# Windowed attention with a gate, decode step: one collecting matmul a pair, sums of probabilities applied once a set, gate inputs accumulated in strided column groups

## The chip, the cores and the metric

The kernel runs on one core of a Trainium2 chip. The metric is device time in microseconds of one execution, here the median of three runs. The profile and the trace come from one further execution, whose own time is in the table below. Five engines work from queues of their own and meet at semaphores: PE (matrix products into PSUM, with PEld for the loading of weights), DVE and ACT (elementwise work and reductions), POOL (a few memsets here) and SP, which issues nearly all loads. All data are 32-bit floats.

## The reference

Two tokens (B = 2, one position each) of width 512. Attention over the last 4096 positions of a cache of 32768, with 32 query heads on 8 key/value heads, and a gated MLP beside it:

```python
x = A_x                                   # (2, 1, 512)
xn = _layernorm(x)
# attention: W = 4096, rep = 4, Dh = 128
q = (xn @ wq).reshape(B, 1, 32, 128).transpose(0, 2, 1, 3)
k = jnp.repeat(k_cache[:, :, Sk - W:, :], 4, axis=1)
v = jnp.repeat(v_cache[:, :, Sk - W:, :], 4, axis=1)
p = _softmax(jnp.einsum("bhqd,bhkd->bhqk", q, k) * 128 ** -0.5)
s = jnp.einsum("bhqk,bhkd->bhqd", p, v).transpose(0, 2, 1, 3).reshape(B, 1, 4096) @ wo
# gate: w_in (512, 1792), halves of 896
z = _gelu(xn @ w_in)
z1, z2 = z[..., :896], _layernorm(z[..., 896:])
g = _silu((z1 * (w_sp * z2 + b_sp)) @ w_out)
return x + s * g
```

## The kernel before

Work goes by *pairs*: a pair is one batch entry and one key/value head, 16 in all (pair n is batch n // 8, head n % 8). A pair needs 2 MB of keys and 2 MB of values. All large loads are issued by SP in the order of use into a ring of nine slots of 16 KB a partition (`slot`): w_in in two halves, w_out, wq in four, then k and v of each pair, then wo in seven blocks. A slot is loaded anew when the matmuls that read it have ended.

Every instruction of PE, DVE, ACT and SP is recorded through one helper (`InOrder`), which keeps the program order of the source on each engine. So the source order is the queue order, and the profile shows nearly everything at line 36, the helper's; groups are told apart by their tiles. A full matmul of 32-bit floats shows as two records in the profile, a transpose on PE as one.

The preamble (lines 85 to 276) normalizes x, makes the gate inputs `z` (lines 182 to 193), turns them (`zT_ps`, lines 198 to 202), computes the gate (lines 218 to 264) with the queries in between, and turns the queries into `qT`.

The loop over pairs (lines 413 to 435) runs three pairs at once: `cur` (keys turned, scores, row maximum), `prev` (exponent, transposed probabilities, product with the values, evacuation) and `old` (collection). In one iteration:

- `bias` and `probs` of prev: the negative maximum (DVE), then the exponent on ACT, which also leaves the row sums `p.l`
- `transposes` of cur: 32 PE transposes of keys into `kt` banks, copied to `kts` by DVE or ACT; between them `probs_t` of prev, two DVE transposes of the probabilities
- `share_sum` and `weights` of prev: PE adds the row sums over partitions, DVE takes the reciprocal and makes four scales `p.w`
- `scores` of cur: 16 matmul passes into four column groups of `s`
- `collect` of old: four matmuls of 128 columns add the parts of the evacuated output `p.o` into `col`, one column group for each 32 of the 128 columns of a head; if the pair is the last of its set, DVE reduces `col` into `o1`
- `pv` of prev, `row_max` and `share_max` of cur, `evacuate` of prev on ACT, with the scales `p.w`

The output projection works on *sets* of heads: set 0 is heads 0 to 3, set 1 heads 4 and 5, set 2 heads 6 and 7, of both batch entries (`SETS`). So set 0 ends with pairs 3 and 11, set 1 with pairs 5 and 13, set 2 with pairs 7 and 15, and `collect` of pair 13 stands in the iteration of pair 15. `spread` brings a finished set into the form `oT` that the product with wo needs: matmuls with 0/1 matrices (`perm8`, `perm16`) and one DVE copy.

After the loop (lines 460 to 495) come, in this order: bias and exponent of pair 15, spread of sets 0 and 1, the DVE transposes of pair 15's probabilities, collection of pair 14, the sums and weights of pair 15, and then alternately the halves of `pv` of pair 15 and the wo blocks, `collect` of pair 15, `spread(2)`, the third wo block, the evacuation `parts` and the last product `so`:

```python
    bias(last)
    probs(last)
    spread(0)
    spread(1)
    probs_t(last, 0)
    probs_t(last, 1)
    collect(old)
    ...
    wo_early(1)
    collect(last)
    spread(2)
    wo_early(2)
```

Of the kernel before, what the change touches and what calls it, by code (L numbers as in the profile page):

```python
# [9 lines left out]
F32 = mybir.dt.float32  # L10
# [4 lines left out]
P = 128  # L15
HQ, DH = 32, 128
G = 4
# [24 lines left out]
def kernel(  # L42
# [38 lines left out]
    def bank(name, *shape):  # L81
        return ps.tile([P, *shape], F32, tag="kt", name=name, bufs=3)
# [82 lines left out]
    heads = cst.tile([P, 32, REP], F32, tag="heads", name="heads")  # L165
    dve.tensor_copy(heads, free_ap(rowm, 0, [[0, 32], [8, REP]]))
# [3 lines left out]
    perm8 = cst.tile([P, 4, 8, 4, 4], F32, tag="perm8", name="perm8")  # L170
    nc.gpsimd.memset(perm8, 0.0)
    for x in range(4):
        dve.tensor_copy(perm8[:, x, :, :, x], free_ap(ident, 0, [[1, 8], [32, 4]]))
    perm16 = cst.tile([P, 2, 16, 4, 2], F32, tag="perm16", name="perm16")
    nc.gpsimd.memset(perm16, 0.0)
    for x in range(2):
        dve.tensor_copy(perm16[:, x, :, :, x], free_ap(ident, 0, [[1, 16], [32, 4]]))
# [3 lines left out]
    assert KT == G  # L181
    z = sb.tile([P, F], F32, tag="kts", name="z")
    for n in range(G):
        pz = bank(f"z{n}", 512)[:, :FC]
        for k in range(KT):
            pe.matmul(
                pz[32 * k : 32 * k + 32, :], xnT[:, k, :], win[k // 2][:, k % 2, n * FC : (n + 1) * FC],
                start=True, stop=True,
            )
        if n % 2:  # L190
            dve.tensor_copy(z[:, n * FC : (n + 1) * FC], pz)
        else:
            act.activation(z[:, n * FC : (n + 1) * FC], pz, AF.Copy)
# [4 lines left out]
    pt = bank("zT_ps", 2, FT, B)  # L198
    zv = z.rearrange("b (h p j) -> b h j p", h=2, j=FT)
# [19 lines left out]
    dve.tensor_copy(zT, pt)  # L219
# [31 lines left out]
    queries(2)  # L251
    y = bank("y", DC)
    for j in range(FT):
        for g in range(G):
            pe.matmul(
                y[32 * g : 32 * g + 32, :], hT[:, j, :], wout[:, j, g * DC : (g + 1) * DC],
                start=(j == 0), stop=(j == FT - 1),
            )
# [31 lines left out]
    for i, (kv, n, nj) in enumerate(SETS):  # L290
        o1 = cst.tile([P, B, 32], F32, tag=f"o1_{i}", name=f"o1_{i}")
# [4 lines left out]
        sets[f"oT{i}"] = (o1, oT, nj)  # L296

# [80 lines left out]
    def collect(p):  # L378
        b, kv = divmod(p.n, HKV)
        a0, n, o1 = sets[kv]  # L380
        if a0 == 0:
            col[b] = ps.tile([P, 4, 32], F32, tag="col", name=f"col{p.n}")
        for a in range(4):
            pe.matmul(
                col[b][32 * a : 32 * a + 32], selw[:, 28 - REP * a0 : 60 - REP * a0], p.o[:, :, 32 * a : 32 * a + 32],
                start=(a0 == 0), stop=(a0 == n - 1),
            )
        if a0 == n - 1:
            dve.reduce_sum(o1[:, b, :], col[b].rearrange("p a j -> p j a"), axis=AX.X)

    def spread(i):
        o1, oT, nj = sets[f"oT{i}"]
        perm = {8: perm8, 16: perm16}[nj]
        nx = 32 // nj
        pt = bank(f"oT_ps{i}", B, nj)
        for x in range(nx):
            pe.matmul(
                pt, perm[:, x].rearrange("p h a x -> p (h a x)"), o1[:, :, nj * x : nj * x + nj],
                start=(x == 0), stop=(x == nx - 1),
            )  # L400
        dve.tensor_copy(oT[:, :, 0 : 16 * B : 16], pt.rearrange("p b j -> p j b"))
# [11 lines left out]
    for cur in pairs:  # L413
# [11 lines left out]
        do(share_sum, prev)  # L425
        do(weights, prev)
# [41 lines left out]
    share_sum(last)  # L468
    weights(last)
# [54 lines left out]
```

## Time and profile before

| | us |
|---|---|
| median of 3 runs | 219.26 (219.24 to 219.27) |
| the profiled execution | 219.47 |
| its span, first to last instruction | 217.6 |
| PE busy | 175.8 (81%) |
| DVE busy | 109.7 (50%) |
| ACT busy | 80.5 (37%) |
| read from HBM | 89.40 MB, mean 411 GB/s over the span |

In the prediction's lines, a timeline row gives start, duration, engine, source line, operation, tiles (out<-in), shapes and a count of merged records; in square brackets stands the idle time of the engine before the row and what ended it. PE's ends are modelled, so starts are the safer times. A row of the chain in order of time gives start, duration and what the chain consisted of. A row of a table by stretches gives, after the stretch and its length, the busy time and the records of PE, PEld, DVE, ACT and POOL, then the granted clock of PE, the share of the DMA engines' time and GB/s.

### The profile page before, as it was taken

How to read it: one execution, taken by the hardware profiler on the slowest of the kernel's cores; microseconds unless marked ns; L12 is line 12 of the kernel's file. 1: busy time of each engine (PE TensorE's matmuls, PEld its weight loads, DVE VectorE, ACT ScalarE, POOL GpSimd, SP SyncE). 2: the span in 40 equal slices, each digit the busy share in tenths (PEclk: the TensorE clock that was granted, in tenths of full speed). 3: DMA queues.
4: the chain of work that ended last, by engine and by line, in shares of the span. 5: the costliest groups of instructions: out<-in, count | busy, mean ns of one | idle time of the engine just before them, and what ended most of it. 6: DMA issues, size and time to landing. Idle time of an engine off the chain costs nothing.

```text
span 217.6 us, 3810 instructions
## 1 busy us (share of the span) xinstructions
PE 175.8 (81%) x1554; PEld 106.3 (49%) x1554; DVE 109.7 (50%) x259; ACT 80.5 (37%) x173; POOL 3.6 (2%) x17
## 2 busy tenths in 40 slices
PE   0479986676997999797977979797986899798963
PEld 0127623436572846455462746456372847464232
DVE  2411225653774557575664747575663557476001
ACT  5011230032373336435363544536363236444210
POOL 6000000000000000000000000000000000000000
PEclk9998599996999699999999999999999699999999
DMA  6999999999999999999999999999999999999980
GB/s 241 428 439 425 434 434 431 431 426 419 428 434 428 434 429 428 431 434 431 434 434 428 431 425 431 434 429 425 425 428 431 431 435 426 431 431 428 423 332 11
DMA packets 6673, 89.64 MB, mean 412 GB/s; under 512 B 750, under 2 KB 766, under 8 KB 1152
## 3 DMA queue, kind: packets, MB, share of 16 engines
q1 hardware_dynamic: 6636, 89.40, 96.6%
q8 instruction: 12, 0.20, 0.3%
q14 instruction: 5, 0.04, 0.0%
q10 hardware_dynamic: 20, 0.01, 0.0%
HBM read 89.40 MB, written 0.00 MB: 411 GB/s over the span
## 4 chain that ended last, share of the span: by engine, by line
DMA 88%; PE 9%; issue 0%; DVE 0%
DMA k<-in_A_k_cache_dram 65%; DMA wq<-in_A_wq_dram 11%; DMA wo<-in_A_wo_dram 9%; PE kt L36 8%; DMA win<-in_B_w_in_dram 3%; PE q_ps L36 1%; DVE res L36 0%; PE so L36 0%; PE mo L36 0%
## 5 line engine op out<-in xcount | busy, mean ns | idle before, releaser
L36 PE MATMUL kt<-ident,k 128*128 128x128 f32 x512 | 69.8, 291 | 19.1 <-DMA k<-in_A_k_cache_dram 19.1
L36 PEld LDWEIGHTS kt<-ident,k 128*128 128x128 f32 x512 | 59.7, 148 | 26.9 <-issue 18.6
L36 DVE COPY kts<-kt 128x512 f32<-128x512 f32 x64 | 42.4, 681 | 30.5 <-PE kt L36 18.3
L36 ACT ACTIVATE kts<-kt 128x512 f32<-128x512 f32 x64 | 36.7, 597 | 37.9 <-PE kt L36 37.9
L36 ACT ACTIVATE o<-acc,wd 128x128 f32<-128x128 f32 x64 | 18.3, 368 | 54.4 <-PE acc L36 37.7
L36 PE MATMUL acc<-v,pT 128*16 128x512 f32 x256 | 30.6, 593 | 0.4 <-DVE pT L36 0.4
L36 PE MATMUL s<-kts,qT 128*32 128x512 f32 x256 | 30.8, 598 | 0.0
L36 DVE TENSOR_REDUCE m<-s 128x1 f32<-128x1024 f32 x16 | 19.6, 1222 | 13.5 <-PE s L36 13.5
L36 DVE STREAM_TRANSPOSE pT<-p 128x512 f32<-128x512 f32 x32 | 20.7, 686 | 0.2 <-ACT p L36 0.2
L36 ACT ACTIVATE p<-s,nb 128x1024 f32<-128x1024 f32 x16 | 18.1, 1133 | 3.7 <-DVE nb L36 3.7
L36 PEld LDWEIGHTS acc<-v,pT 128*16 128x16 f32 x256 | 7.8, 108 | 10.7 <-issue 10.3
L36 PEld LDWEIGHTS mo<-mg,same 128*128 128x128 f32 x32 | 4.8, 188 | 15.9 <-DVE mg L36 15.9
L36 PEld LDWEIGHTS s<-kts,qT 128*32 128x32 f32 x256 | 6.6, 108 | 10.0 <-ACT kts L36 7.9
L36 PE MATMUL q_ps<-wq,xnT 128*32 128x512 f32 x64 | 9.0, 687 | 1.7 <-DMA wq<-in_A_wq_dram 1.7
L36 PE MATMUL z<-win,xnT 128*32 128x448 f32 x32 | 7.2, 907 | 2.8 <-DMA win<-in_B_w_in_dram 2.8
L36 PEld LDWEIGHTS col<-o,selw 128*32 128x32 f32 x128 | 4.1, 110 | 9.0 <-issue 8.7
L36 DVE TENSOR_REDUCE o<-col 128x32 f32<-128x128 f32 x6 | 1.8, 292 | 12.4 <-PE col L36 12.4
L36 PE MATMUL mo<-mg,same 128*128 128x4 f32 x32 | 6.2, 263 | 2.1 <-DVE mg L36 1.6
L36 DVE TENSOR_REDUCE nb<-mo 128x1 f32<-128x4 f32 x16 | 2.6, 162 | 9.9 <-PE mo L36 9.9
L36 PE MATMUL part<-wo,oT 128*32 128x512 f32 x48 | 5.7, 596 | 1.4 <-DMA wo<-in_A_wo_dram 1.3
L36 PE MATMUL zT_ps<-rowm,z 128*128 128x2 f32 x28 | 6.6, 370 | 0.0
L36 PEld LDWEIGHTS zT_ps<-rowm,z 128*128 128x128 f32 x28 | 6.5, 325 | 0.0
(98 smaller groups left out, 82.1 us busy)
## 6 DMA issues: line engine op xcount, KB each, us to landing
k<-in_A_k_cache_dram SPq DMA_DIRECT2D x16, 2048.0 KB, 34.6
v<-in_A_v_cache_dram SPq DMA_DIRECT2D x16, 2048.0 KB, 36.1
wq<-in_A_wq_dram SPq DMA_DIRECT2D x4, 2048.0 KB, 21.1
wo<-in_A_wo_dram SPq DMA_DIRECT2D x3, 2048.0 KB, 33.7
win<-in_B_w_in_dram SPq DMA_DIRECT2D x2, 1792.0 KB, 9.1
wout<-in_B_w_out_dram SPq DMA_DIRECT2D x1, 1792.0 KB, 14.8
wo<-in_A_wo_dram SPq DMA_DIRECT2D x1, 1024.0 KB, 32.2
wo<-in_A_wo_dram SPq DMA_DIRECT2D x1, 512.0 KB, 28.9
```

The costliest lines, as they stand in the source:

```text
L36: return self.tc.keep_in_program_order(call(*args, **kwargs))
```

## The change

- **Sums of probabilities once a set.** `share_sum` and `weights` are gone. The exponent leaves its row sums in a column of `lsum`. `evacuate` scales by the constant selector `diag`. A new function `normalize`, called by `collect` at the last pair of a set, adds the sums of all the set's pairs with one matmul, reduces `col`, picks each head's sum, takes the reciprocal and scales `o1`.
- **One collecting matmul a pair.** `collect` issues one matmul of 512 columns into 32 rows of `col` in place of four of 128 into four column groups. `o1` is now (heads of the set) x batch x 128; the reduction over the four parts reads 512 elements a row and writes 128.
- **Spreading.** One matmul of 256 columns with a fan-out matrix, two DVE products with a selector (`own`), and one DVE reduction of 256 elements replace the `perm` matmuls and the copy.
- **Gate.** `z` is accumulated over the four parts of x in PSUM, in four column groups whose columns are strided by 7 in w_in; one ACT evacuation; four PE transposes in place of 14 matmuls; two copies into `zT`. `y` takes 7 matmuls of 512 columns, an evacuation and 4 matmuls with `rowm`, in place of 28 of 128.

```diff
@@ gate inputs
-    for n in range(G):
-        pz = bank(f"z{n}", 512)[:, :FC]
-        for k in range(KT):
+    z = sb.tile([P, P, 4], F32, tag="kts", name="z")
+    pz = bank("z_ps", 512)
+    for k in range(KT):
+        for g in range(G):
+            first = FH * (g // 2) + (FT - 4) * (g % 2)
             pe.matmul(
-                pz[32 * k : 32 * k + 32, :], xnT[:, k, :], win[k // 2][:, k % 2, n * FC : (n + 1) * FC],
-                start=True, stop=True,
+                pz[32 * g : 32 * g + 32, :], xnT[:, k, :], free_ap(win[k // 2], F * (k % 2) + first, [[FT, P], [1, 4]]),
+                start=(k == 0), stop=(k == KT - 1),
             )
...
+    act.activation(z.rearrange("p q j -> p (q j)"), pz, AF.Copy)
...
-    for h in range(2):
-        for j in range(FT):
-            pe.matmul(pt[:, h, j, :], zv[:, h, j, :], rowm[:, :B], start=True, stop=True)
+    pt = bank("zT_ps", 4, P)
+    for j in range(4):
+        pe.transpose(pt[:, j, :], z[:, :, j], ident)
@@ output of the gate
+    yp = bank("yp", D)
+    for j in range(FT):
+        g = j % G
+        pe.matmul(yp[32 * g : 32 * g + 32, :], hT[:, j, :], wout[:, j, :], start=(j < G), stop=(j >= FT - G))
+    ys = sb.tile([P, D], F32, tag="o", name="ys")
+    act.activation(ys, yp, AF.Copy)
     y = bank("y", DC)
-    for j in range(FT):
-        for g in range(G):
-            pe.matmul(
-                y[32 * g : 32 * g + 32, :], hT[:, j, :], wout[:, j, g * DC : (g + 1) * DC],
...
+    for g in range(G):
+        pe.matmul(y[32 * g : 32 * g + 32, :], rowm, ys[:, g * DC : (g + 1) * DC], start=True, stop=True)
@@ probabilities
-        p.l = sb.tile([P, 1], F32, tag="l", name=f"l{p.n}")
...
-            bias=p.nb, scale=SCALE, accum_out=p.l,
+            bias=p.nb, scale=SCALE, accum_out=lsum[:, p.n : p.n + 1],
...
-    def share_sum(p):
-        pe.matmul(p.mo[:, G : G + 1], heads.rearrange("p a h -> p (a h)"), p.l, start=True, stop=True)
-
-    def weights(p):
-        w = sb.tile([P, 1], F32, tag="w", name=f"w{p.n}")
-        dve.reciprocal(w, p.mo[:, G : G + 1])
-        p.w = sb.tile([P, 4], F32, tag="wd", name=f"wd{p.n}")
-        dve.tensor_scalar_mul(p.w, diag, w)
@@ evacuate
-            act.activation(p.o[:, jj, :], acc[:, jj, :], AF.Copy, scale=p.w[:, jj : jj + 1])
+            act.activation(p.o[:, jj, :], acc[:, jj, :], AF.Copy, scale=diag[:, jj : jj + 1])
@@ collect
-        for a in range(4):
-            pe.matmul(
-                col[b][32 * a : 32 * a + 32], selw[:, 28 - REP * a0 : 60 - REP * a0], p.o[:, :, 32 * a : 32 * a + 32],
-                start=(a0 == 0), stop=(a0 == n - 1),
-            )
+        pe.matmul(
+            col[b][:32].rearrange("p a d -> p (a d)"), selw[:, 28 - REP * a0 : 60 - REP * a0],
+            p.o.rearrange("p a d -> p (a d)"), start=(a0 == 0), stop=(a0 == n - 1),
+        )
         if a0 == n - 1:
-            dve.reduce_sum(o1[:, b, :], col[b].rearrange("p a j -> p j a"), axis=AX.X)
+            normalize(p.n, n, o1)
+
+    def normalize(last, n, o1):
+        b, m = last // HKV, n * REP
+        pl = bank(f"l{last}", n)
+        pe.matmul(
+            pl[:32], heads.rearrange("p a h -> p (a h)"), lsum[:, last + 1 - n : last + 1], start=True, stop=True
+        )
+        dve.reduce_sum(o1[:, b, :], col[b][:m].rearrange("p a d -> p d a"), axis=AX.X)
+        lm = sb.tile([m, n], F32, tag=f"lm{n}", name=f"lm{last}")
+        dve.tensor_mul(lm, pl[:m], diag[:m, :n])
+        w = sb.tile([m, 1], F32, tag=f"w{n}", name=f"w{last}")
+        dve.reduce_sum(w, lm, axis=AX.X)
+        dve.reciprocal(w, w)
+        dve.tensor_scalar_mul(o1[:, b, :], o1[:, b, :], w)
@@ spread
-        for x in range(nx):
-            pe.matmul(
-                pt, perm[:, x].rearrange("p h a x -> p (h a x)"), o1[:, :, nj * x : nj * x + nj],
-                start=(x == 0), stop=(x == nx - 1),
-            )
-        dve.tensor_copy(oT[:, :, 0 : 16 * B : 16], pt.rearrange("p b j -> p j b"))
+        nx = DH // nj
+        pt = bank(f"oT_ps{i}", B, nx, nj)
+        pe.matmul(
+            pt.rearrange("p b x j -> p (b x j)"), fan[nx].rearrange("p h x -> p (h x)"),
+            o1.rearrange("p b d -> p (b d)"), start=True, stop=True,
+        )
+        t = sb.tile([P, B, nx, nj], F32, tag="fan", name=f"fan_{i}")
+        for b in range(B):
+            dve.tensor_mul(t[:, b], pt[:, b], free_ap(own[nx], 0, [[1, nx], [0, nj]]))
+        dve.reduce_sum(oT[:, :, 0 : 16 * B : 16], t.rearrange("p b x j -> p j b x"), axis=AX.X)
```

In the loop and after it, the calls of `share_sum` and `weights` are dropped; the order of the other calls is the same.

More of the change, by code (lines that the diff above doesn't have):

```diff
@@ L164 @@
     dve.tensor_copy(same, free_ap(rowm, 0, [[0, G], [1, 32]]))
-    heads = cst.tile([P, 32, REP], F32, tag="heads", name="heads")
-    dve.tensor_copy(heads, free_ap(rowm, 0, [[0, 32], [8, REP]]))
+    heads = cst.tile([P, 8, REP], F32, tag="heads", name="heads")
+    dve.tensor_copy(heads, free_ap(rowm, 0, [[0, 8], [8, REP]]))
     diag = cst.tile([P, 4], F32, tag="diag", name="diag")
@@ L169 @@
     dve.tensor_reduce(selw[:, 28:32], free_ap(rowm, 0, [[1, REP], [4, 4]]), axis=AX.X, op=ALU.add)
[L170 to L182, printed above, removed]
-    for n in range(G):
-        pz = bank(f"z{n}", 512)[:, :FC]
-        for k in range(KT):
+    fan, own = {}, {}
+    for nx in (8, 16):
+        fan[nx] = cst.tile([P // nx, P // nx, nx], F32, tag=f"fan{nx}", name=f"fan{nx}")
+        dve.tensor_copy(fan[nx], free_ap(ident[: P // nx], 0, [[1, P // nx], [0, nx]]))
+        own[nx] = cst.tile([P, nx], F32, tag=f"own{nx}", name=f"own{nx}")
+        dve.tensor_reduce(own[nx], ident.rearrange("p (h x) -> p x h", x=nx), axis=AX.X, op=ALU.add)
+    assert G == 4 and 4 < FT < 9
+    z = sb.tile([P, P, 4], F32, tag="kts", name="z")
[3 more added lines that the diff above has]
+            first = FH * (g // 2) + (FT - 4) * (g % 2)
             pe.matmul(
-                pz[32 * k : 32 * k + 32, :], xnT[:, k, :], win[k // 2][:, k % 2, n * FC : (n + 1) * FC],
-                start=True, stop=True,
-            )
[L190 to L193, printed above, removed]
+                pz[32 * g : 32 * g + 32, :], xnT[:, k, :], free_ap(win[k // 2], F * (k % 2) + first, [[FT, P], [1, 4]]),
+                start=(k == 0), stop=(k == KT - 1),
+            )
+    act.activation(z.rearrange("p q j -> p (q j)"), pz, AF.Copy)
     wb_ps = ps.tile([P, 512], F32, tag="mo", name="wb_ps")[:, :2]
@@ L218 @@
     zT = cst.tile([P, 2, FT, B], F32, tag="zT", name="zT")
-    dve.tensor_copy(zT, pt)
+    for m, j0, j1 in ((0, 0, 4), (1, 4, FT)):
+        src = free_ap(pt, 32 * m + P * (j0 - (FT - 4) * m), [[64, 2], [P, j1 - j0], [1, B]])
+        dve.tensor_copy(zT[:, :, j0:j1, :], src)
     u = cst.tile([P, 2, FT, B], F32, tag="u", name="u")
@@ L381, in collect @@
         if a0 == 0:
-            col[b] = ps.tile([P, 4, 32], F32, tag="col", name=f"col{p.n}")
-        for a in range(4):
-            pe.matmul(
-                col[b][32 * a : 32 * a + 32], selw[:, 28 - REP * a0 : 60 - REP * a0], p.o[:, :, 32 * a : 32 * a + 32],
-                start=(a0 == 0), stop=(a0 == n - 1),
-            )
-        if a0 == n - 1:
-            dve.reduce_sum(o1[:, b, :], col[b].rearrange("p a j -> p j a"), axis=AX.X)
+            col[b] = ps.tile([P, 4, DH], F32, tag="col", name=f"col{p.n}")
```

14 lines of the change are left out of this document (2 added, 12 removed).

## The prediction

> **What bounds the kernel now.** I read the chain of waits first, on the page and then in order of time, because it says which work ended last at each moment.
>
> ```profile
> DMA 88%; PE 9%; issue 0%; DVE 0%
> ...
> q1 hardware_dynamic: 6636, 89.40, 96.6%
> q8 instruction: 12, 0.20, 0.3%
> ```
>
> ```profile
> 153.05 35.68 DMA k<-in_A_k_cache_dram
> 188.73 0.14 issue
> 188.86 4.14 PE kt L36 x32
> ...
> 213.51 0.04 issue
> 213.55 0.47 PE so L36 x8
> ```
>
> The load queue fills 96.6% of its engines' time, and the chain is loads but for short pieces. So work saved in the sixteen pairs is worth nothing by itself: the same 89.40 MB must still come. What can move the end is the stretch after the last keys landed at 188.73 (pair 15). From there the compute has one pass through scores, probabilities, values, collection and output, while the last loads (v15 and the blocks of wo) still arrive until 213.51. I therefore read the timeline of each engine from 188.86, PE first.
>
> ```profile
> 188.86 4.14 PE L36 MATMUL kt<-ident,k 128*128 128x128 f32 x32 [1.32 <-DMA k<-in_A_k_cache_dram]
> 192.84 0.28 PE L36 MATMUL mo<-l,heads 128*128 128x1 f32 x2
> 193.05 1.92 PE L36 MATMUL s<-kts,qT 128*32 128x512 f32 x16
> 194.79 0.40 PE L36 MATMUL col<-o,selw 128*32 128x128 f32 x8
> 195.01 1.90 PE L36 MATMUL acc<-v,pT 128*16 128x512 f32 x16
> 197.01 0.39 PE L36 MATMUL mo<-mg,same 128*128 128x4 f32 x2
> ...
> 200.01 1.07 PE L36 MATMUL acc<-v,pT 128*16 128x512 f32 x8 [0.36 <-DVE pT L36]
> 200.90 1.90 PE L36 MATMUL part<-wo,oT 128*32 128x512 f32 x16
> 202.62 1.04 PE L36 MATMUL acc<-v,pT 128*16 128x512 f32 x8
> 203.78 1.92 PE L36 MATMUL part<-wo,oT 128*32 128x512 f32 x16
> 205.52 0.40 PE L36 MATMUL col<-o,selw 128*32 128x128 f32 x8
> 206.33 1.06 PE L36 MATMUL oT_ps<-o,perm 128*128 128x16 f32 x8 [0.41 <-DVE o L36]
> 208.72 1.92 PE L36 MATMUL part<-wo,oT 128*32 128x512 f32 x16 [1.33 <-DMA wo<-in_A_wo_dram]
> ...
> 211.66 1.71 PE L36 MATMUL so<-wo,oT 128*32 128x128 f32 x56
> 213.55 0.43 PE L36 MATMUL so<-wo,oT 128*32 128x128 f32 x8 [0.18 <-DMA wo<-in_A_wo_dram]
> ```
>
> ```profile
> 195.26 0.29 DVE L36 TENSOR_REDUCE o<-col 128x32 f32<-128x128 f32 x1 [1.40 <-PE col L36]
> 195.47 1.22 DVE L36 TENSOR_REDUCE m<-s 128x1 f32<-128x1024 f32 x1
> 196.72 0.23 DVE L36 TENSOR_SCALAR mg<-grpm,m 128x4 f32<-128x4 f32 x1
> 197.43 0.16 DVE L36 TENSOR_REDUCE nb<-mo 128x1 f32<-128x4 f32 x1 [0.48 <-PE mo L36]
> 197.62 0.15 DVE L36 TENSOR_SCALAR nb<-nb 128x1 f32<-128x1 f32 x1
> ...
> 199.25 1.31 DVE L36 STREAM_TRANSPOSE pT<-p 128x512 f32<-128x512 f32 x2 [0.21 <-ACT p L36]
> ...
> 214.04 0.29 DVE L36 TENSOR_TENSOR res<-so,gate 128x128 f32<-128x128 f32 x1 [6.36 <-PE so L36]
> ```
>
> ```profile
> 196.98 1.14 ACT L36 ACTIVATE o<-acc,wd 128x128 f32<-128x128 f32 x4 [3.34 <-DVE mg L36]
> 197.99 1.13 ACT L36 ACTIVATE p<-s,nb 128x1024 f32<-128x1024 f32 x1
> ```
>
> The slack of this stretch is what the change must not use up. Pair 15's second half of values starts at 202.62, and its eight passes issue in 0.89 (200.01 to 200.90), so PE was free at 203.51 and stood 0.27 until 203.78. At 208.72 it stood 1.33 for wo. The 56 passes of so from 211.66 are seven blocks of eight; eight passes took 0.22 elsewhere (194.79 to 195.01), so the last block could have gone at 211.66 + 7 x 0.22 = 213.20 and waited 0.35. Together 0.27 + 1.33 + 0.35 = 1.95 us.
>
> **The change part by part.** Removed from every pair: the sum of shares on PE (0.21, from 192.84 to 193.05), the reciprocal and the scaling on DVE (two small operations), and three of four collecting matmuls. None of it ended a wait of the load queue, so by itself it gives nothing before pair 15.
>
> *The preamble* (gate inputs, four turning transposes, y in two steps) ends under the loads: PE waits for keys at every pair, 19.1 us over the kernel.
>
> ```profile
> L36 PE MATMUL kt<-ident,k 128*128 128x128 f32 x512 | 69.8, 291 | 19.1 <-DMA k<-in_A_k_cache_dram 19.1
> L36 PE MATMUL zT_ps<-rowm,z 128*128 128x2 f32 x28 | 6.6, 370 | 0.0
> L36 PE MATMUL z<-win,xnT 128*32 128x448 f32 x32 | 7.2, 907 | 2.8 <-DMA win<-in_B_w_in_dram 2.8
> ```
>
> The turning falls from 28 passes (6.6 us) to 4; the 32 passes of z now read with a stride, which no row shows. Even at twice 7.2 us they add about what the turning gives back. I count 0; with the cover gone the preamble would be worth -6 to +1. Gate is used only at 214.04.
>
> *The collecting matmul.* A call is two records here (64 calls, x128). Before, eight passes of 128 columns over four column groups took 0.22. Now two passes of 512 columns run in one group. Sixteen 512-column passes over four groups go from 200.90 to 202.62: 1.72, four rounds of 0.43. A lone pass costs at least a quarter of a round, 0.11, and at most a round. The 32 transposes, one at a time, take 4.14 for 128 columns each, 0.13, or 0.52 for 512, so I take the whole round: 2 x 0.43 = 0.86 (bounds 0.22 and 1.04). The Trainium skill, "TensorE: Matmul & The Clock Gate", section "Back-to-back issue gap", gives 216 ns for 512 columns; by it the matmul would cost 0.43, each of the two on the path below would be 0.43 cheaper, and the sum would be +0.3 instead of +1.2. The rounds of 0.43 at full clock speak against it.
>
> *Normalizing once a set* is the new work on DVE: a reduction of 512 elements in place of 128, then four small dependent operations. Between 0.29 for 128 elements and 1.22 for 1024 the line gives 0.69 for 512 (bounds 0.29 and 1.22). DVE takes the next independent operation about 0.08 before the end (195.26 + 0.29 against 195.47). Small dependent ones follow at 0.19 (197.43 to 197.62). It stands in collect, which the program puts ahead of the row maximum, and the set of pair 13 ends in the iteration of pair 15. So:
>
> Scores of pair 15 start at 192.84 (no sum of shares), 0.21 earlier. Collection at 194.58; its result after 0.86 + 0.18 (0.40 less 0.22) = 195.62, and 0.07 later (195.19 to 195.26) DVE starts at 195.69. Reduction 0.61, three small ones 0.57, scaling 0.15: row maximum at 197.02 instead of 195.47, +1.55. Everything to the bias follows: 197.77 becomes 199.32. ACT starts the exponent at 199.37 instead of 197.99, since the evacuation of pair 14 no longer holds it; the probabilities are ready 1.26 later (197.99 to 199.25), at 200.63.
>
> *Spreading* was two matmul groups and two copies of about 0.2, done while ACT worked. Now DVE has for each of sets 0 and 1 two products of 128x128 from PSUM (0.29 each, started 0.21 apart) and a reduction of 256 elements (0.29 + 128 x 1.04 ns = 0.42; next start 0.35): 0.21 + 0.29 + 0.03 + 0.35 = 0.88 a set, 1.76 for both, and they stand ahead of the transposes of pair 15's probabilities, which are queued on the same engine. From 199.47, when PE's product is there, they last until 201.23. That is later than 200.63, so the transposes start at 201.23 instead of 199.25: +1.98.
>
> PE waits behind that: values at 201.99, the first wo block at 202.88, second half at 204.60, free at 205.49 (203.51 + 1.98). The second wo block landed long ago; it goes at 205.49 and takes 1.74 (203.78 to 205.52). Collection of pair 15 at 207.23; 1.04 + 0.07 to DVE, 0.61 + 0.57 + 0.23 for the normalizing, 0.05 to PE: spreading at 209.80. Its two passes of 256 columns take 0.43 to 0.55. The third wo block starts at 210.26 instead of 208.72: +1.54, and wo's wait there is gone. From here nothing is changed: the last block of so would go at 213.20 + 1.54 = 214.74. The loads ended at 213.51, so PE decides: 214.74 - 213.55 = **+1.2 us**. In one line: the transposes are 1.98 late; from collection to spreading it takes 2.57 instead of 0.81 (205.52 to 206.33), +1.76; the spreading itself 0.5 instead of 1.06 (206.33 to 208.72 less 1.33), -0.56. That is 3.18, less 1.95 of slack.
>
> One assumption stands in it: that pair 15 still starts at 188.86. A plain iteration grows by 0.86 - 0.22 - 0.21 = 0.43; pair 13 also carries the normalizing of pair 11, about 1.5. Against these 2 to 2.4 us stand the 1.32 that PE waited at 188.86 and a late start two pairs earlier:
>
> ```profile
> 169.50 5.35 PE L36 MATMUL kt<-ident,k 128*128 128x128 f32 x32 [2.54 <-DMA k<-in_A_k_cache_dram]
> ```
>
> ```profile
> 170.00:174.00 4.00, 4.00 (x24) 4.00 (x22) 3.00 (x5) 1.20 (x3) 0.00 (x0) 0.57 1.01 434
> ```
>
> Pair 13 waited 2.54 for its keys and then ran at a granted clock of 0.57, 5.35 instead of 4.14. With less idle time before it PE keeps its clock and has 1.2 more: the start is kept. If not, 2.4 less 1.32 leave up to 1 us by which pair 15 starts later; that is the upper end.
>
> **The rivals.** *Later still*: pair 13 is as slow as before (1.0), or the two reductions of 512 cost their upper bound (2 x 0.53 = 1.1). Either gives +2.2 to +2.3, 221.5. For it: no row shows a reduction that strides over 512 elements, and none shows whether the clock holds.
>
> *The added work stays under the loads*: if a lone pass costs a quarter of a round, collection is 0.64 cheaper twice, the added 3.18 shrink to 1.9 and just fit in the 1.95. The time is 219.2 to 219.4, no change. The same comes out if keys of pair 15 land earlier. Instruction loads are 0.20 MB for 3108 PE records, 64 B each. 188 matmul passes and as many weight loads go away (zT 24, y 34, sums 20, collecting 96, spreading 14): 24 KB of 196. In the trace such a load went out at 164 to 165, before the late keys at 169.50:
>
> ```profile
> q8 instruction: 1, 0.02, 5.5%
> ```
>
> With fewer and later ones the last keys could land up to 1.2 earlier (2.54 less the usual 1.32), and +1.2 becomes 0. I think they land as before, as only one or two of the twelve fall away. The Trainium skill says, in "Runtime: NRT & Kernel Launch", section "Instruction fetch mechanics", that the instructions come in 16 KiB blocks over a DMA queue of the engine; the twelve of 0.02 MB agree.
>
> *Faster*: both together, and the engines' uneven end shrinks:
>
> ```profile
> 212.00:213.00 1.00, 1.00 (x48) 0.98 (x41) 0.00 (x0) 0.00 (x0) 0.00 (x0) 1.00 0.16 59
> ```
>
> Between 212 and 213 the 16 engines are busy 0.16 of the time on the mean: a few of them end late. If the latest end 0.5 earlier and the compute fits, the time is 218.8. Against it: the compute has only 0.35 in hand there.
>
> **How the numbers follow.** The profiled execution took 219.47 us for a span of 217.6 and the median is 219.26, 0.21 less; the difference is carried over: 219.26 + 1.2 = 220.45. Chances: forecast 0.55 (own range 219.8 to 221.1), later still 0.20, under the loads 0.17, faster 0.08. What a measurement of this kernel tells from no change is taken as 0.2%, 0.44 us. Some of the under-the-loads case ends just over that: slower 0.77, same 0.15, faster 0.08. The range of 8 in 10 is 219.3 to 221.7.
>
> **What would show it.** In the changed profile: the row maximum of pair 15 starts more than 1 us after its scores; six DVE operations stand between bias and transposes; the third wo block follows the spreading at once, with no wait for wo; the last pieces of the chain are PE, DVE and ACT instead of one long wo load. I am wrong if PE still waits for wo at its last block, if pair 15 starts a us earlier, or if the collecting pass takes 0.1 rather than 0.4.

## The result and the profile after

The changed kernel takes 227.72 us (226.88 to 228.58, 4 runs); the kernel before, on the same chip, 219.26. The ratio is 1.0347, 95% interval 1.0297 to 1.0397. The direction was forecast, the size was not: +8.5 us against +1.2. The profiled execution after took 228.58 us for a span of 226.8.

From the page of the changed kernel, its clock row, its load queues and the shares of the chain of waits:

```profile
PEclk9996788796999999999999999999999999985958
...
q1 hardware_dynamic: 6636, 89.40, 93.4%
q8 instruction: 11, 0.18, 0.3%
...
DMA 77%; PE 17%; DVE 3%; issue 1%; ACT 0%; DVEq 0%; ACTq 0%
```

The same bytes are loaded, but the queue's share has fallen from 96.6% to 93.4%, and PE and DVE now stand in the chain where loads stood before. New, and in no step of the prediction, are the fives near the end of the clock row. The chain in order of time says where the chain leaves the loads (start, duration, what):

```profile
154.36 36.54 DMA k<-in_A_k_cache_dram
190.90 0.14 issue
191.04 4.14 PE kt L36 x32
...
206.70 3.27 PE part L36 x16
...
215.66 2.74 PE part L36 x16
...
219.13 4.11 PE so L36 x72
223.26 0.30 DVE res L36
223.59 0.29 DVE res L36
```

From 191.04 on there is no load in it. Two things are to be seen. Pair 15 starts at 191.04, not at 188.86: 2.18 us are lost before the stretch of the prediction begins. And pieces that nobody changed are longer: a wo block took 1.72 us to issue before and takes 3.27 here; the 72 passes of so take 4.11, where before they took 2.57 with a wait for the last load in it (211.41 to 213.98). The PE timeline of the changed kernel shows what they stand behind:

```profile
191.04 4.14 PE L36 MATMUL kt<-ident,k 128*128 128x128 f32 x32 [2.27 <-DMA k<-in_A_k_cache_dram]
195.11 1.92 PE L36 MATMUL s<-kts,qT 128*32 128x512 f32 x16
196.85 1.02 PE L36 MATMUL col<-o,selw 128*32 128x512 f32 x2
197.71 0.17 PE L36 MATMUL l<-lsum,heads 128*32 128x2 f32 x1
...
200.78 0.39 PE L36 MATMUL mo<-mg,same 128*128 128x4 f32 x2 [1.13 <-DVE mg L36]
201.09 1.13 PE L36 MATMUL oT_ps<-o,fan 16*128 16x256 f32 x4
...
204.79 1.91 PE L36 MATMUL acc<-v,pT 128*16 128x512 f32 x8 [1.39 <-DVE pT L36]
206.47 3.49 PE L36 MATMUL part<-wo,oT 128*32 128x512 f32 x16
...
214.99 0.67 PE L36 MATMUL oT_ps<-o,fan 8*128 8x256 f32 x2 [1.56 <-DVE o L36]
215.59 2.78 PE L36 MATMUL part<-wo,oT 128*32 128x512 f32 x16
```

PE now waits three times for DVE after the scores (1.13, 1.39, 1.56), where before the largest such wait was 0.41; behind the second and the third it is slow. A table by stretches of 3.41 us, the step in which the granted clock changes in the records, has it (PE, PEld, DVE, ACT, POOL busy, then the granted clock, the share of the DMA engines, GB/s). First one stretch of the kernel before, then three of the changed kernel:

```profile
202.86:206.28 3.42, 2.94 (x32) 0.68 (x24) 0.29 (x1) 1.14 (x4) 0.00 (x0) 1.00 0.99 424
```

```profile
199.45:202.86 3.41, 2.28 (x12) 1.10 (x8) 2.48 (x7) 2.34 (x6) 0.00 (x0) 1.00 1.02 432
202.86:206.28 3.42, 2.03 (x9) 0.35 (x12) 2.36 (x6) 0.00 (x0) 0.00 (x0) 0.50 0.99 422
206.28:209.69 3.41, 3.41 (x20) 0.74 (x16) 0.00 (x0) 0.00 (x0) 0.00 (x0) 0.50 0.98 402
```

So the traces name three candidates: the forecast serial work, keys that land later, and a clock of 0.50 in parts of the end (202.86 to 209.69, and again from 216.52). DVE's own rows answer to those of before:

```profile
197.91 0.68 DVE L36 TENSOR_REDUCE o<-col 8x128 f32<-8x512 f32 x1 [2.21 <-PE l L36]
...
199.25 1.20 DVE L36 TENSOR_REDUCE m<-s 128x1 f32<-128x1024 f32 x1
...
201.83 0.49 DVE L36 TENSOR_TENSOR fan<-oT_ps,own 128x128 f32<-128x128 f32 x2 [0.27 <-PE oT_ps L36]
202.42 0.59 DVE L36 TENSOR_REDUCE oT<-fan 128x32 f32<-128x256 f32 x1
202.92 0.48 DVE L36 TENSOR_TENSOR fan<-oT_ps,own 128x128 f32<-128x128 f32 x2
203.50 0.61 DVE L36 TENSOR_REDUCE oT<-fan 128x16 f32<-128x256 f32 x1
204.03 1.29 DVE L36 STREAM_TRANSPOSE pT<-p 128x512 f32<-128x512 f32 x2
```

### The profile page after: what moved, and what is told of

It is laid out like the page before. It is cut to its first block, busy times and chain, and to the rows that moved or that the text cites. A ratio compares the mean times of both kernels' runs of the same rounds, so it can differ in the third digit from the quotient of the medians.

```text
span 226.8 us, 3413 instructions
## 1 busy us (share of the span) xinstructions
PE 182.0 (80%) x1366; PEld 94.3 (42%) x1366; DVE 112.2 (49%) x254; ACT 80.8 (36%) x173; POOL 2.9 (1%) x15
## 3 DMA queue, kind: packets, MB, share of 16 engines
q1 hardware_dynamic: 6636, 89.40, 93.4%
HBM read 89.40 MB, written 0.00 MB: 394 GB/s over the span
## 4 chain that ended last, share of the span: by engine, by line
DMA 77%; PE 17%; DVE 3%; issue 1%; ACT 0%; DVEq 0%; ACTq 0%
DMA k<-in_A_k_cache_dram 64%; DMA wq<-in_A_wq_dram 10%; PE kt L36 7%; PE part L36 3%; DMA win<-in_B_w_in_dram 3%; PE so L36 2%; PE acc L36 1%; PE q_ps L36 1%; DVE o L36 1%; PE s L36 1%; PE col L36 1%; PE oT_ps L36 1%; DVE oT L36 1%; DVE m L36 1%; DVE fan L36 0%
## 5 line engine op out<-in xcount | busy, mean ns | idle before, releaser
L36 PEld LDWEIGHTS kt<-ident,k 128*128 128x128 f32 x512 | 58.5, 146 | 19.0 <-PE mo L36 7.6
L36 ACT ACTIVATE o<-acc,diag 128x128 f32<-128x128 f32 x64 | 18.2, 368 | 65.6 <-PE acc L36 65.6
L36 PE MATMUL acc<-v,pT 128*16 128x512 f32 x256 | 39.1, 611 | 1.4 <-DVE pT L36 1.4
L36 PE MATMUL q_ps<-wq,xnT 128*32 128x512 f32 x64 | 10.2, 765 | 9.1 <-DMA wq<-in_A_wq_dram 9.1
L36 PEld LDWEIGHTS acc<-v,pT 128*16 128x16 f32 x256 | 9.0, 112 | 18.5 <-issue 16.0
L36 PE MATMUL col<-o,selw 128*32 128x512 f32 x32 | 16.6, 599 | 0.0
L36 DVE TENSOR_REDUCE o<-col 8x128 f32<-8x512 f32 (+1 forms) x6 | 4.1, 679 | 19.2 <-PE l L36 19.2
L36 PE MATMUL part<-wo,oT 128*32 128x512 f32 x48 | 8.2, 812 | 0.0
L36 PEld LDWEIGHTS q_ps<-wq,xnT 128*32 128x32 f32 x64 | 1.9, 121 | 12.7 <-DMA wq<-in_A_wq_dram 9.5
L36 PE MATMUL z_ps<-win,xnT 128*32 128x512 f32 x32 | 5.7, 845 | 0.9 <-DMA win<-in_B_w_in_dram 0.9
```

Source lines behind the costliest of these rows:

```text
L36: return self.tc.keep_in_program_order(call(*args, **kwargs))
```

## The experiments

Ratios are to the kernel before on the same chip. That kernel's own times fall into groups near 219.4, 220.5 and 221.6 in these runs, so small differences are read from ratios with their intervals.

### The parts alone

The changed kernel once more:

> The changed kernel as it is, beside the kernel before on one chip. Its first profile had the keys of pair 15 at 190.90 instead of 188.73, load packets of 16 KB at 614 to 620 ns instead of 611, and PE at half clock in two stretches of the end. Theory A (serial work at the end, made dear by the clock): 3 to 3.5% slower again, with the clock at 0.5 somewhere after 200 us. Rival B (the loads themselves became slower through the change): packets again above 611 ns here while those of the kernel before on the same chip are 611, and pair 15 again about 2 us late.

Measured: 229.09 us (226.04 to 229.91), ratio 1.0312 (1.0193 to 1.0432). The size is no accident of one run. Its trace has both signs again: half clock from 204.42 and from 218.07, and pair 15 at 191.12.

The kernel before with the gate part of the change alone (`z`, `zT`, `y`):

```diff
-        for k in range(KT):
...
+    for k in range(KT):
+        for g in range(G):
...
+        pe.transpose(pt[:, j, :], z[:, :, j], ident)
```

> The kernel before with the gate part of the change alone (strided accumulation, four turning transposes, y in two steps). Theory A: the preamble ends under the loads, so 0 (within 0.3 us of before). Rival C (the emptier preamble or the strided reading costs): 1 to 2 us slower. Rival B in the form that the strided reading disturbs the loads: 1.5 us slower with longer packets.

Measured: 219.36 us, ratio 0.9978 (0.9938 to 1.0018). The preamble costs nothing, as the prediction counted it; the cause is in the rest of the change: the collection, its sums, the spreading, and the constant tiles that they need.

### The clock in the end

The changed kernel with filler matmuls of 128 x 128 in PE's three waits:

```diff
+    def warm(name, n):
+        t = bank(name, 512)
+        for i in range(n):
+            pe.matmul(t[:, :P], ident, ident, start=True, stop=True)
...
+        if cur.n == NP - 1:
+            warm("warm_a", 3)
...
+    warm("warm_b", 4)
...
+    warm("warm_c", 5)
```

> The changed kernel with filler matmuls (128x128 by 128 columns, results unused) on PE in three places where it waits at the end: 3 before the shared maximum of pair 15, 4 before its values, 5 before the last spreading; together some 3 us of PE work inside waits of 1.13, 1.39 and 1.56 us. Theory A: PE keeps its clock, the wo blocks take 1.72 to 1.9 instead of 3.3 and 2.7, the last product about 2.2 instead of 4.1, and the time falls by 4 to 5 us, to within about 1.5% of before. Rival (the clock is a by-product and the waits alone make the time): no change or slower by the fillers.

Measured: 224.44 us (223.18 to 224.80), ratio 1.0169 (1.0100 to 1.0237). The medians put it 4.65 below the changed kernel on the same chip, the ratios 1.4%, or 3.1 us, with intervals that overlap; two more pairs with and without fillers stand below, and their intervals do not. More work on PE made the kernel faster: in the trace its clock stays at 1.0 until PE's last matmul. The PE timeline with the fillers, where a wo block takes 1.90 again:

```profile
204.52 1.06 PE L36 MATMUL acc<-v,pT 128*16 128x512 f32 x8 [0.50 <-DVE pT L36]
205.41 1.90 PE L36 MATMUL part<-wo,oT 128*32 128x512 f32 x16
```

The changed kernel with the collection of pair 13 and the spreads behind pair 15's transposes:

```diff
-        do(collect, old)
+        if cur.n < NP - 1:
+            do(collect, old)
+        else:
+            late = old
...
-    spread(0)
-    spread(1)
     probs_t(last, 0)
     probs_t(last, 1)
-    collect(old)
+    spread(0)
+    collect(late)
...
+    spread(1)
+    collect(old)
```

> The changed kernel with another order at the end: the collection of pair 13 leaves the iteration of pair 15 and stands after the transposes of pair 15's probabilities; the values of pair 15 follow the transposes at once; spreading and the other collection stand behind the first wo block. Same operations, same counts. Theory A: the added DVE work goes under the wo blocks, PE waits for wo again at its end, time within 0.5% of before. Rival B (loads slower) or C (preamble): still 1% or more slower.

Measured: 223.38 us (221.90 to 224.66), ratio 1.0128 (1.0041 to 1.0216). That is above the 0.5% expected. Of PE's three waits the first is gone, the second is 1.15, and the third, before the last spreading, stays whole; the clock falls there alone. Its PE timeline:

```profile
211.26 0.66 PE L36 MATMUL oT_ps<-o,fan 8*128 8x256 f32 x2 [1.57 <-DVE o L36]
211.85 2.60 PE L36 MATMUL part<-wo,oT 128*32 128x512 f32 x16
```

### Why the keys land later

In all these traces of changed kernels but that of the gate part, the 16 KB packets of the loads took longer. The change has other constant tiles, and in the built programs the ring's slots begin 32 bytes higher in a partition: at 32544 after, at 32512 before. Four runs change only that (the fourth, `aligned512`, follows further below):

```diff
# aligned: the changed kernel with 32 bytes more
-    lsum = cst.tile([P, B * HKV], F32, tag="lsum", name="lsum")
+    lsum = cst.tile([P, B * HKV + 8], F32, tag="lsum", name="lsum")
# shifted: the kernel before with its slots at 32544
-    grpm = cst.tile([P, G], F32, tag="grpm", name="grpm")
+    grpm = cst.tile([P, 16], F32, tag="grpm", name="grpm")[:, :G]
# aligned128: as aligned, with + 24 columns; aligned512: with + 56
```

> The changed kernel with 32 bytes a partition more in the tile of the sums, nothing else. In every kernel with the change's own constants the load packets of 16 KB took 614 to 621 ns, in the kernel before and in the one with the gate part alone 611. The change's smaller and larger constant tiles move the nine load slots from byte 32512 of a partition (a multiple of 64) to 32544 (32 above one); here they begin at 32576, a multiple of 64. Theory B2 (the slots' start decides the packets' time): packets 611, keys of pair 15 near 189, time 1.5 to 2.2 us below the changed kernel. Rival (other traffic or accesses of the change slow the loads): packets still 614 to 621.

> The kernel before with one small constant tile 32 bytes a partition larger, so that the load slots begin at byte 32544, 32 above a multiple of 64, as in the changed kernel. All else as before. Theory B2: packets 614 to 621, keys of pair 15 about 1.5 us later, time 1.2 to 2 us (0.6 to 0.9%) above before. Rival: packets 611 and no change.

> The changed kernel with 96 bytes more in the tile of the sums: the slots begin at byte 32640, a multiple of 128 but not of 256. If a multiple of 128 is enough, the 16 KB packets take 611 ns; if 256 is needed, 613 to 621 ns as with the start at 32576. The time is between 224.5 and 229 us either way, as the half clock in the end decides it.

Measured: `aligned` 227.24 us, ratio 1.0323 (1.0264 to 1.0383), no cure; `aligned128` 229.72 in its one run, no cure either. `shifted` 221.81 us, ratio 1.0086 (1.0041 to 1.0131): a 32-byte step of the buffers alone costs the kernel before 1.9 us by the ratio. Durations of the 16 KB load packets, from the traces, and the start of the slots:

```
kernel       slots from   mod 256   mean ns   commonest ns (packets)
before       32512        0         612.5     611 (4960)
gate alone   32512        0         612.5     611 (4961)
shifted      32544        32        617.1     614 (2712), 621 (1054)
after        32544        32        616.9     614 (2702), 621 (1060)
aligned      32576        64        615.9     613 (2446), 620 (976)
aligned128   32640        128       615.7     611 (1456), 613 (633), 615 (540)
aligned512   32768        0         612.3     611 (4961)
```

Only the starts at a multiple of 256 give 611 for nearly all of the 4992 packets. The Trainium skill, "DMA: Bandwidth & Descriptors", section "How a descriptor splits into AXI transactions", says that a transaction must start at a 256-byte boundary, and that a descriptor which starts elsewhere begins at the boundary below it and pays for the bytes in between. The table agrees that the boundary of 256 matters (means of 615.7 to 617.1 ns off it, 612.3 to 612.5 on it), but the page speaks of bytes that are fetched, while here the start that moved is the one that the load writes. A mean of 616.9 instead of 612.5 is 0.7%, or 1.4 of 190 us; why pair 15 starts 1.8 later in `shifted` (190.70) and 2.2 later in the changed kernel is not settled beyond that.

The PE timeline of `shifted` shows the later start, and that in this execution the old kernel's last wo block ran slowly too. It waited hardly longer than before (1.38 against 1.33), but PE was busy for only 1.62 of the 3.41 us stretch around that wait, and the next stretch had half clock:

```profile
190.70 4.13 PE L36 MATMUL kt<-ident,k 128*128 128x128 f32 x32 [1.42 <-DMA k<-in_A_k_cache_dram]
...
210.57 3.37 PE L36 MATMUL part<-wo,oT 128*32 128x512 f32 x16 [1.38 <-DMA wo<-in_A_wo_dram]
```

With fillers, and with fillers and the reordered end:

> The changed kernel with both: the slots at a multiple of 64 and the filler matmuls in three waits of PE at the end. Theory A + B2: what is left is the serial work at the end alone, with PE at full clock: +1.2 to +2.5 us above before (220.5 to 222), as the prediction had summed it without the clock and the slots. Against aligned, the fillers alone then give 3 to 5 us. Rival: more than 1.5% above before, so a further cost is hidden.

> The changed kernel with the slots at a multiple of 64, the other order at the end (collection of pair 13 and the spreading behind the transposes of pair 15), and two groups of filler matmuls. Theory A + B2: within 0.4% of before, PE waiting for wo at one of its last blocks. Rival (what is left is in the operations, not in their place): still 1% or more slower.

Measured: 224.27 us, ratio 1.0195 (1.0155 to 1.0235), and 221.87 us, ratio 1.0100 (1.0052 to 1.0148). Both are above what was expected (up to 222 us, and within 0.4% of before): the packets were still long (615.9 in `aligned`), so these are fillers and reordering with late loads. Against `aligned` the fillers alone give 2.97 us, and here the intervals do not overlap. The slots at a multiple of 512:

> The changed kernel with 224 bytes more in the tile of the sums (columns that nothing uses), so that the ring's slots begin at byte 32768 of a partition, a multiple of 512. Theory B2 (the start of the slots lengthens the load packets; the 32-byte step to a multiple of 64 was not enough): the 16 KB packets go back to 611 ns, the keys of pair 15 land near 189 us instead of 190.5 to 190.9, and the time falls by 1.5 to 2 us, to about 226 us, since the half clock in the end stays. Rival (the packets are longer for another reason that the change brings): 613 to 621 ns as before and the time of the changed kernel, 227 to 229 us.

> As the one before, with the twelve filler matmuls in TensorE's three waits (their results are used by nothing). Both added causes are then gone and the prediction's sum stands alone: theory A's added serial steps on VectorE of 1.2 us, or with the spreads as they were measured (1.1 to 1.2 us a set instead of 0.88) up to 2.5 us: 220.5 to 222 us. If there is a fourth cause, 223 us or more.

> As the one before, with the collection of pair 13 and the spreads moved behind the transposes of pair 15. By theory A the serial steps are now covered, so the time is within 0.4% of before: 218.8 to 220.3 us. If moving work does not take it off the chain, it stays at 220.5 to 222 us.

Measured: `aligned512` 226.93 us, ratio 1.0336 (1.0281 to 1.0390), where 226 was expected. The packets are back at 611 and pair 15 starts at 189.35, 1.7 earlier, and its profiled run is 1.56 shorter (227.02 against 228.58). But the medians differ by 0.8 and the ratios by 0.1%, so over all runs a gain from the slots is not shown here. With the fillers, 222.32 us (221.56 to 223.08), ratio 1.0115 (1.0057 to 1.0172): 4.6 below `aligned512`, well clear of it, and 1.95 below `aligned_warm` (0.8% by the ratios, whose intervals still overlap a little). With the reordered end too, 221.04 us, ratio 1.0056 (1.0000 to 1.0111), a little above the 0.4% expected; in the profiled run pair 15's transposes ran at half clock (5.35 instead of 4.14).

That last effect is in other runs too. A split of each profiled execution at the start of pair 15 takes it and the other causes apart (start of pair 15, duration of its transposes, and time from that start to the end of DVE's last operation, all from the timelines):

```
kernel            start     transposes   start to end
before            188.86    4.14         25.80
aligned512_warm   189.13    4.14         27.71
warm              190.77    4.14         27.70
aligned_warm      190.59    5.44         29.01
aligned512        189.35    4.14         32.84
after             191.04    4.14         32.84
aligned           190.51    5.45         31.86
```

`aligned_warm` lost 1.3 us to its transposes, which is no cost of late keys in itself; only 1.46 of its distance to `aligned512_warm` is the start. And `aligned` had half clock in its transposes, but later only once (204.54 to 211.36), where `aligned512` had it twice: in these executions that is why its late loads do not show in its time. `aligned512_warm`, `aligned512_reorder_warm` and, below, `fan_full` and `fan_full_reorder` have times in two groups 1.2 to 1.5 us apart, and each profiled execution lies in the longer group just where its transposes took 5.35; that this makes the groups in the executions without a trace is likely and not shown.

`aligned512_warm` is the kernel in which the prediction's sum stands alone. Its PE timeline:

```profile
189.13 4.14 PE L36 MATMUL kt<-ident,k 128*128 128x128 f32 x32 [1.78 <-DMA k<-in_A_k_cache_dram]
...
198.87 0.39 PE L36 MATMUL mo<-mg,same 128*128 128x4 f32 x2 [0.26 <-DVE mg L36]
...
202.89 1.07 PE L36 MATMUL acc<-v,pT 128*16 128x512 f32 x8 [0.51 <-DVE pT L36]
...
210.69 0.67 PE L36 MATMUL oT_ps<-o,fan 8*128 8x256 f32 x2 [0.26 <-DVE o L36]
211.28 1.92 PE L36 MATMUL part<-wo,oT 128*32 128x512 f32 x16
213.98 0.43 PE L36 MATMUL so<-parts,rowm 128*32 128x128 f32 x8 [0.78 <-ACT parts L36]
```

### What about the change lets the clock fall

The fillers show that more work keeps the clock, not what took it. The spreading matmul over all 128 rows (the sets and `fan` padded with zeros), and, as its rival, the collecting matmul over all 128 columns of weights; both with slots at a multiple of 512:

```diff
# fan_full
-        fan[nx] = cst.tile([P // nx, P // nx, nx], F32, tag=f"fan{nx}", name=f"fan{nx}")
+        fan[nx] = cst.tile([P, P // nx, nx], F32, tag=f"fan{nx}", name=f"fan{nx}")
+        nc.gpsimd.memset(fan[nx], 0.0)
...
-        o1 = cst.tile([n * REP, B, DH], F32, tag=f"o1_{i}", name=f"o1_{i}")
+        o1 = cst.tile([P, B, DH], F32, tag=f"o1_{i}", name=f"o1_{i}")
+        nc.gpsimd.memset(o1, 0.0)
# col_wide512
-            col[b][:32].rearrange("p a d -> p (a d)"), selw[:, 28 - REP * a0 : 60 - REP * a0],
+            col[b].rearrange("p a d -> p (a d)"), selw[:, 28 - REP * a0 : 156 - REP * a0],
```

> The changed kernel with slots from byte 32768, and with the spreading matmul over all 128 rows: the finished sets and the fan-out matrices have 128 partitions, zero but for the 8 or 16 that are used. Duration of every step is meant to stay. Theory C (the clock counts a matmul by the rows of the array that it uses, so the 8- and 16-row spreading counts for next to nothing): weighted by rows, PE works 0.43 and 0.39 of the two windows of 3.41 us before the clock halves in the run with slots from 32768, and no window above 0.48 is followed by half clock but one; with 128 rows these windows come to 0.71 and 0.56, the clock stays at 1.0, and the time falls by up to 4.6 us from 226.9, to 222 to 223.5 us. Rival C2 (the waits alone halve it) and C3 (the collecting matmul's 32 columns count too little): no change, 226.5 to 228 us.

> The changed kernel with slots from a multiple of 512, and with the collecting matmul over all 128 columns of weights (96 of them zero) instead of 32. Theory C3 (columns count): the window with a collecting matmul keeps the clock, 222 to 225 us. Theory C (rows count) and C2 (the waits alone): half clock as before, 226.5 to 228 us.

Measured: `fan_full` 221.34 us (221.12 to 222.66, 10 runs), ratio 1.0060 (1.0026 to 1.0094). That is below the 222 to 223.5 expected. Without a filler, with nearly the same waits and durations of the spreading, 5.6 us of the time of `aligned512` are gone (226.93 less 221.34, on different chips; 2.8% by the ratios). `col_wide512` 225.28 us (224.95 to 225.98), ratio 1.0234 (1.0191 to 1.0277): below what theory C expected and just above what C3 did, with one stretch at half clock in each place where `aligned512` has two. Whether columns count a little, or the stretches only fell more kindly, is left open. Stretches of `aligned512`, then of `fan_full` (columns as above):

```profile
198.50:201.91 3.41, 2.42 (x8) 1.10 (x8) 2.38 (x10) 1.90 (x5) 0.00 (x0) 1.00 1.02 437
201.91:205.33 3.42, 2.23 (x12) 0.56 (x16) 1.73 (x3) 0.00 (x0) 0.00 (x0) 0.50 0.96 412
```

```profile
200.27:203.69 3.42, 2.21 (x8) 0.92 (x8) 2.82 (x9) 1.21 (x2) 0.00 (x0) 1.00 1.04 446
203.69:207.10 3.41, 3.17 (x32) 1.05 (x36) 0.78 (x2) 0.00 (x0) 0.00 (x0) 1.00 0.94 394
```

By the busy column `fan_full` worked less (2.21 against 2.42) and kept its clock. Of the 2.42, 1.06 are the spreading with 16 and 8 of 128 rows. Counted by rows they are 0.10, the stretch has 2.42 - 0.96 = 1.46 of 3.41, or 0.43, and the next one is granted half. In `fan_full` all of the 2.21 count, 0.65. Its PE timeline has the old durations behind these waits, though its transposes ran at half clock in this execution (222.58 us, of the longer group):

```profile
189.20 5.35 PE L36 MATMUL kt<-ident,k 128*128 128x128 f32 x32 [2.12 <-DMA k<-in_A_k_cache_dram]
...
203.93 1.06 PE L36 MATMUL acc<-v,pT 128*16 128x512 f32 x8 [1.45 <-DVE pT L36]
204.82 1.90 PE L36 MATMUL part<-wo,oT 128*32 128x512 f32 x16
...
211.73 0.67 PE L36 MATMUL oT_ps<-o,fan 128*128 128x256 f32 x2 [1.56 <-DVE o L36]
212.33 1.92 PE L36 MATMUL part<-wo,oT 128*32 128x512 f32 x16
```

The same with the reordered end and no fillers:

> The version with 128 rows in the spreading, and the collection of pair 13 and the spreads moved behind the transposes of pair 15, with no filler matmuls. If theory C holds: within 0.8% of before, 219.3 to 221 us, as the same order with fillers (221.04). If it does not: 222 to 224 us, as the half clock falls on the last wo block and the last product (reordered without fillers: 223.4).

Measured: 220.47 us (220.02 to 221.81, 10 runs), ratio 1.0018 (0.9985 to 1.0051): the time of before, with the whole change in it and within the 219.3 to 221 expected. In its PE timeline the first passes of so start 1.3 us later than before (212.74 instead of 211.41): the last collection, normalizing and spreading cannot be moved. With so's wait for its last load gone, the profiled run took 220.30 us against 219.47:

```profile
209.43 0.67 PE L36 MATMUL oT_ps<-o,fan 128*128 128x256 f32 x2 [1.56 <-DVE o L36]
210.03 1.92 PE L36 MATMUL part<-wo,oT 128*32 128x512 f32 x16
212.74 0.43 PE L36 MATMUL so<-parts,rowm 128*32 128x128 f32 x8 [0.78 <-ACT parts L36]
```

No version beats the kernel before: its loads fill the time, and the change saves nothing of them.

## Why the prediction was right in its direction and wrong in its size

In the profiled executions the loss splits cleanly by the table above: 2.18 us from the later start of pair 15 (191.04 less 188.86), 1.91 from the serial work at full clock (27.71 less 25.80), and 5.13 from the clock (32.84 less 27.71). Together they are 9.22, and the two executions are 9.11 apart; the medians, 8.5, are a little closer together. The forecast had the second alone.

**The serial sum, 1.2 us: its mechanism held, and one term was too small.** Taken from `aligned512_warm`, relative to the start of pair 15: the row maximum's product moves from 8.15 (197.01 - 188.86) to 9.74 (198.87 - 189.13), +1.59 where +1.55 was forecast. The values start at 13.76 instead of 11.15, +2.61 where +1.98 was forecast. Collection to spreading takes 2.63 (208.06 to 210.69), forecast 2.57; spreading to the third wo block 0.59, forecast 0.5; from that block to the first res 4.94 (211.28 to 216.22), the forecast 4.48 + 0.47. The term that missed most is the spreading: 0.88 a set was taken, 1.1 was measured (201.83 to 202.92, 202.92 to 204.03 in the changed kernel), since the reduction of 256 elements takes 0.59 to 0.62, not 0.42. That makes 0.45 of the 0.63; the other 0.18 had gone by before the spreading began. I had drawn the line through two reductions that read PSUM. Steps alone are not the reason: the reduction of 512 in collect steps too, also reads PSUM, and came on the line (0.68 for 0.69). The one that missed reads SBUF with steps, and the trace of before had a price for that. The first of these two rows steps through SBUF, the second does not:

```profile
1.65 0.37 DVE L36 TENSOR_REDUCE rowm<-ident 128x32 f32<-128x128 f32 x1 [1.65 <-POOL ident masks.py:199]
1.94 0.28 DVE L36 TENSOR_REDUCE grpm<-ident 128x4 f32<-128x128 f32 x1
```

With 0.09 more for 128 elements, an estimate from these rows for 256 is 0.42 + 0.18 = 0.60. No run changed the steps or the memory of that reduction alone, so this is likely and not shown. With 0.63 more before the values, 0.15 from the two smaller terms and 0.27 from a later start the 1.2 become 2.2; the profiled run of `aligned512_warm` ends 2.1 above that of before (221.56 against 219.47).

**"That pair 15 still starts at 188.86": failed, but not for the reason weighed.** I asked whether PE would be late; PE waits for the keys even longer (2.27). The loads themselves are slower, because the change's constant tiles take 32 bytes more and move the slots. "The same 89.40 MB must still come" is right and was taken for the same time. Price: 2.18 us in the profiled run; 1.9 by `shifted` against before, where the start is 1.84 later. The longer packets account for about 1.4 of it, and the rest is open.

**"From here nothing is changed": the step that failed most.** Every duration after 191 was carried over at full clock. I had quoted a row in which pair 13 ran at 0.57 after a wait of 2.54, and used it only for pair 13, while the same sum made three new waits on PE and replaced 1.06 and 1.49 us of spreading over 128 rows by 0.67 and 1.13 over 8 and 16. Price: 5.13 us in the profiled run. In the medians it is 4.6 by the fillers and 5.6 by the padded rows, both against `aligned512`, but 3.0 by the fillers against `aligned`: it depends on where the stretches of 3.41 us fall. The sum of +1.2 was off sevenfold, yet its direction did not come by luck, since its own mechanism alone gives +1.9.

**What came as forecast.** The preamble at nothing (0.9978). The collecting pass at a whole round, 2 x 0.43 = 0.86 (196.85 to 197.71); the 216 ns for 512 columns that I weighed against it, from the Trainium skill, "TensorE: Matmul & The Clock Gate", section "Back-to-back issue gap", are not what one of these 32-bit passes takes. The reduction of 512 at 0.68 for 0.69. Six DVE operations between bias and transposes, no wait for wo before the third block, and a chain that ends in PE, DVE and ACT.

**The rivals.** "Later still" put the clock in doubt, but for pair 13, and ended at 221.5. "Under the loads" rested on a pass at a quarter of a round, which took a whole one, or on keys that land earlier, and "faster" on both; the keys landed 2.2 later. Fewer instruction loads (11 for 12) brought nothing that shows.

## What to carry to other kernels

Before a duration is carried over from the old trace, ask what clock it ran at, and count PE's work in each stretch of 3.41 us, by the rows of the array that a matmul uses: new waits together with matmuls over few rows can cost more than the work that they replace. Zero rows that fill the contraction up to 128 cost no time here and kept the clock. And look where the large load buffers begin after any edit of the small tiles: a start off a multiple of 256 bytes made the mean 16 KB packet longer.

## What the runs showed of the hardware

- **The clock and the rows of the array.** `fan_full` shows that in these kernels the work that keeps the clock is not plain busy time: the same spreading over 128 rows kept it, and over 8 and 16 rows lost it. In 17 traces there are 886 stretches of 3.41 us at full clock, from 25 us on. Counted by plain busy time, nine of the 56 that are followed by half clock had PE busy for 0.55 to 0.84 of the time, while others at 0.42 to 0.55 kept it. Counted by rows, every stretch above 0.53 kept the clock but one (0.84, in the run of the gate part, unexplained), and every one below 0.46 lost it but two (0.415 and 0.418). Between 0.46 and 0.53 both occur, so the bound of 0.48 that I expected before `fan_full` was drawn too sharply; whether columns count too is open. The Trainium skill, "TensorE: Matmul & The Clock Gate", Part 1, section "What's actually happening", tells of a free-running window of 3413 ns and of half clock after an idle window; the step of 3.41 us agrees, but here stretches with 2.3 to 2.4 us of matmuls were followed by half clock.
- **32 bytes.** A start of the load buffers off a multiple of 256 bytes lengthens the mean 16 KB packet from 612.5 to between 615.7 and 617.1 ns; with 32 bytes, the kernel before became 1.9 us slower (`shifted`, ratio 1.0086).
- **A reduction that steps through SBUF.** 128 elements a partition took 0.37 us with steps and 0.28 without (`rowm`, `grpm`), and 256 with steps 0.59 to 0.62, where the line through reductions from PSUM gives 0.42. From PSUM, 512 elements with steps took 0.68, on that line.
